# One weight load moved ahead, one chunk's inverse a step later, two periods interleaved, a fourth head product in the last down stage

## The chip, the cores and the metric

The kernel runs on one core of a Trainium2 chip. Its engines work side by side, each through its own queue of instructions in order: TensorE (PE, with PEld for the weight loads), VectorE (DVE), ScalarE (ACT), GpSimd (POOL) and SyncE (SP), which issues the DMA transfers here. The metric is the device time of one execution in microseconds; the time of a kernel is the median of its runs.

## The reference

One layer of a transformer with a spectral mixer, on 8192 tokens of 448 channels. What is computed, cut to its core:

```python
mod = (_silu(c) @ w_mod).reshape(c.shape[0], 6, 1, -1)
sa, ca, ga, sb, cb, gb = (mod[:, n] for n in range(6))
h = _layernorm(x) * (1 + ca) + sa
x = x + ga * spectral(h, w1, b1, w2, b2)   # rfft2 over 1 x 8192, two block-diagonal
                                           # complex layers (4 blocks of 112) with ReLU and
                                           # a soft threshold, irfft2
h = _layernorm(x) * (1 + cb) + sb
x = x + gb * ((_gelu(h @ w_gate) * (h @ w_up)) @ w_down)   # 448 -> 1792 -> 448
```

## The kernel before

**Stages.** The 8192 tokens are 64 rows of 128; the transform is built as 128 x 64 matmuls. The first stage does the modulation, the norm, the forward transform, the two spectral layers and the first half of the inverse transform, whose result goes to memory (`vd<-us`). Everything behind it goes by chunks of two rows (`CB = 2`, 256 tokens), 32 in all. For each chunk there is an `inverse` (second half of the inverse transform; its `v` comes from memory and is split into two parts for the matmul from chunk 3 on, `split_v`), a `residual` with `x`, `stats2`, `rsqrt_part`, `norm2`, `pack` (a cast into two f16 parts) and transposes, and then the feed-forward part.

**Chunks 0 to 7** (`NSTD = 8`) take `NFT = 14` steps of `gate_up` (L1127) each; after every two steps a row of the product gate times up goes through a sum of blocks on POOL (L1176 to L1179) and `quantize` (ACT L1187 for the high f16 part, DVE L1188 for the low). `down(i - 1)` runs inside step 2 of chunk `i`. It is Strassen's seven products of half matrices, each over `NP = 7` tile rows and each with three matmuls per row (high by high, high by low, low by high: L1200 to L1202). While these chunks run, the rows of the down weights are prepared: `load_d8(t)` loads row `t` by three DMAs into a tile `dr`, `down_hi(t)` (ACT, L948) and `down_lo(t)` (DVE, L952) make the two f16 parts `wds[t]`.

**Chunks 8 to 31** use a fast form of the gate and up products too, whose weights `wk` are made on the way and stored to memory. Here the work goes by periods `u`, from `U0 = 56`, seven for a chunk. A period has the matmul stages `stage_a`, `stage_b`, `stage_c` and `stage_d` (all L1362), with `copy_b` (ACT L1390: a result of `stage_a` out of PSUM, on which `stage_b` needs to wait), `seed` (ACT L1394), `gel`, `mult`, `sums` and `quant` steps behind them. `phase` puts a chunk's inverse (`winverse`, L1472 to L1474) and the `down` of the chunk before into one of the seven periods.

**What sets the order.** The kernel is written out by hand: the order of the instructions of each engine is the order of the calls. Tables say which calls stand behind which step: `hooks` (steps 0 to 13 of a chunk, for the chunk one or two later), `second` (chunk 1's own additions), `first` (chunk 0 and, by running step number, what follows), `opening` and `late` (first periods; last `down`). `at(n, "load", ...)` puts a load at step `n` of the first stage. All transfers go through the one SP queue, in order.

**Places that the change touches.** Between the first stage and chunk 0 lies a transition: `inverse(0)`, `residual(0)`, `stats2(0)`, `down_hi(0)`, the Sqrt of `rsqrt0` (L1055) with five small DVE operations (L1057 to L1061), `norm2` (L1076, L1077), `pack_hi`, `pack_lo`, and eight transposes on PE (L1109), then the first `gate_up`. Ahead of it `drain()` ends the first stage, some pools are closed and the pool `cp` is opened in their space: in it lie `n2` (the target of `norm2`), `pk` and the tiles `wds[1]` to `wds[6]`. After `down_lo(0)` the pool `fp` is closed, in whose space `cq` and `cp2` (the homes of `dr`) are opened. At the other end, the last `down` has nothing behind it that PE could do: it works off three head products in cuts of tile rows 0 to 3, 4 and 5, with `late` calls (the last period's `stage_d`, `gel1`, `sums`, `quant`) after each cut, and then the rest.

Of the kernel before, what the change touches and what calls it, by code (L numbers as in the profile page):

```python
# [19 lines left out]
D = 448  # L20
# [4 lines left out]
CB = 2  # L25
# [24 lines left out]
def spectral_geglu(ctx, tc, x, w1, b1, w2, b2, wg, wu, wd, cvec, wmod, cf1, cs2, cmi, cgm, out):  # L50
# [277 lines left out]
    with ExitStack() as bctx:  # L328
# [225 lines left out]
        def at(i, hook, fn, *args):  # L554
            side.setdefault((i, hook), []).append((fn, args))
# [346 lines left out]
        def load_d(t, a, b):  # L902
            dma(a[:, 0:2], wdp[t][:, :, 0:HC])
            dma(a[:, 2], wdp[t][:, 1, HC:])
            dma(b, sd[t])
            draws[t] = a, b
# [66 lines left out]
        at(31, "load", load_v1)  # L973
        for i in range(17, nu - 1):
            step(i)
# [5 lines left out]
    with ExitStack() as cctx:  # L981
        cp = cctx.enter_context(tc.tile_pool(name="cp", bufs=1, side="right"))
        H = 128 * CB
        nxt[0]["n"] = cp.tile([128, CB, D], F32, tag="n2", name="n2")
        pkt = cp.tile([128, NXT * 128], F16, name="pk")
# [10 lines left out]

        def load_d8(t):
            load_d(t, *(cp2.tile([128, n, HC], F32, tag=f"dr{n}", name="dr", bufs=2) for n in (3, 4)))
# [377 lines left out]
        def stage_b(u):  # L1376
            mm(u, RY, S2, T2)
# [69 lines left out]
        def period(u):  # L1447
            on(u, stage_a)
            on(u - 1, seed)
            for fn, *args in held:  # L1450
                fn(*args)
            held.clear()
            on(u - 2, joins)
            on(u - 2, gel3)
            on(u - 4, quant_lo)
            on(u - 2, mult3)
            on(u, copy_b)
# [7 lines left out]
            on(u, stage_b)  # L1465
            on(u, lambda v: after(v, 0))
# [172 lines left out]
        for n, k in enumerate((4, 7, 11, 13)):  # L1639
# [15 lines left out]

        second = {
# [32 lines left out]
            5: [(down_hi, 3)],  # L1689
            6: [(down_lo, 3), (load_d8, 5)],  # L1690
            7: [(down_hi, 4)],
            8: [(down_lo, 4), (load_d8, 6)],
            9: [(down_hi, 5)],
            10: [(down_lo, 5)],
            12: [(down_hi, 6)],
            13: [(down_lo, 6)],
# [8 lines left out]
        S.copy(ga_r[:, HC:], ga[:, HC:D])  # L1705
        down_lo(0, range(1))
# [12 lines left out]
        cq = cctx.enter_context(tc.tile_pool(name="cq", bufs=1))  # L1719
        cctx2 = ExitStack()  # L1720
# [8 lines left out]
        V.tensor_scalar(gb_r, gb_r, ds_d, None, op0=ALU.mult)  # L1729

# [12 lines left out]
        for i in range(NSTD):  # L1743
# [4 lines left out]
            for k in range(NFT):  # L1748
# [3 lines left out]
                if k % 2 == 1 and i + k > 1:  # L1752
                    quantize(*((i, k // 2 - 1) if k > 1 else (i - 1, NP - 1)))
# [25 lines left out]
        quantize(NSTD - 1, NP - 1)  # L1779
# [27 lines left out]
        for u in range(U0, NT_ + 1):  # L1807
# [17 lines left out]
            0: lambda: [on(NT_ - 1, joins), on(NT_ - 1, gel3), on(NT_ - 3, quant_lo), on(NT_ - 1, mult3), on(NT_ - 1, stage_d), on(NT_ - 1, gel1), on(NT_ - 1, mult1), on(NT_ - 2, quant_hi), sums(xs[NT_ - 1], V)],  # L1825
# [79 lines left out]
```

## Time and profile before

| | |
|---|---|
| median of 3 runs | 1902.98 us (1902.56 to 1904.65) |
| profiled execution | 1900.89 us, of it the span 1899.1 us |
| mean granted clock of TensorE | 0.994 |
| first stage | 0 to about 367 us |
| transition | about 367 to 382 us (first `gate_up` at 382.35) |
| chunks 0 to 7 | to about 766 us |
| periods | about 766 to 1877 us |
| last `down` | about 1877 us to the end |

The stage bounds are read from the timeline by the first instruction of `gate_up`, of `stage_a` and of the last `down`. The time of the profiled execution lies 1.79 us above its span, for what the span does not hold. Times in rows are microseconds from the start of the span. A row of a timeline has the start, the duration, the engine, the line, the operation, output and inputs with their shapes, and in brackets the idle time of the engine just before with what ended it.

### The profile page before, as it was taken

The page shows a single profiled execution, that of the slowest core. Times are in us where ns is not written, and L with a number is a line of the kernel's source. Part 1 is how long each engine was busy: PE and PEld are TensorE (multiplying, and loading weights), DVE is VectorE, ACT ScalarE, POOL GpSimd, SP SyncE. Part 2 cuts the span into 40 slices and gives each one's busy share as a digit, 9 for nine tenths or more (in the row PEclk, how much of TensorE's full clock was granted, in tenths as well). Part 3 has the DMA queues.
Part 4 walks back from the last instruction along what each step waited for, and adds up shares of the span by engine and source line. Part 5 has one row for each costly group of instructions (what it writes and reads, how often), then busy time and mean ns, then how long its engine had stood idle before and what let it go on. Part 6 is the DMA issues. An engine that isn't in the chain of part 4 may idle for free.

```text
span 1899.1 us, 56360 instructions
## 1 busy us (share of the span) xinstructions
PE 1853.8 (98%) x23332; PEld 1754.4 (92%) x23332; DVE 1429.7 (75%) x2888; ACT 994.8 (52%) x1844; POOL 1265.3 (67%) x1616
## 2 busy tenths in 40 slices
PE   7899999899999999999999999999999999999998
PEld 3599999878989889899999999999999999999998
DVE  8677788777666667777777777777777777777645
ACT  5687888653444444345554545555454454444443
POOL 3157654256777778677777777777777777777533
PEclk9999999999999999999999999999999999999999
DMA  9999777644543445966666666556666666666651
GB/s 356 316 293 262 204 177 196 183 136 108 127 109 89 104 95 128 270 178 175 176 176 168 167 167 167 167 167 168 172 177 174 169 175 179 173 176 175 155 151 55
DMA packets 380602, 330.49 MB, mean 174 GB/s; under 512 B 110772, under 2 KB 358712, under 8 KB 380344
## 3 DMA queue, kind: packets, MB, share of 16 engines
q1 hardware_dynamic: 380344, 326.87, 62.6%
q8 instruction: 183, 3.00, 0.6%
q14 instruction: 75, 0.61, 0.1%
HBM read 243.32 MB, written 60.10 MB: 160 GB/s over the span
## 4 chain that ended last, share of the span: by engine, by line
PE 80%; DVE 8%; DMA 4%; ACT 3%; SPq 2%; issue 2%; POOL 1%; ACTq 0%; DVEq 0%; POOLq 0%
PE set L1362 37%; PE pgu L1127 11%; PE pdn L1202 6%; PE pdn L1200 6%; PE pdn L1201 6%; PE ps L211 2%; DVE y L472 2%; PE set L1201 2%; PE set L1202 2%; PE set L1200 2%; DVE wk L827 1%; PE set L1472 1%; ACT th L114 1%; DVE st L172 1%; DMA tr<-td 0%
## 5 line engine op out<-in xcount | busy, mean ns | idle before, releaser
L1362 PE MATMUL set<-nt,wk 128*128 128x128 f16 x13104 | 743.9, 220 | 5.6 <-ACT sb L1390 4.2
L1362 PEld LDWEIGHTS <-wk 128*128 128x128 f16 x13104 | 736.9, 98 | 10.5 <-issue 8.2
L1202 PE MATMUL pdn<-wd,ac 128*128 128x224 f16 x1218 | 316.1, 260 | 1.2 <-DVE ac L1437 1.2
L1200 PE MATMUL pdn<-wd,ac 128*128 128x224 f16 x1218 | 316.3, 260 | 0.6 <-ACT ac L1427 0.6
L1201 PE MATMUL pdn<-wd,ac 128*128 128x224 f16 x1218 | 316.1, 260 | 0.0
L1127 PE MATMUL pgu<-nt,wk 128*128 128x256 f16 (+1 forms) x2464 | 270.1, 275 | 4.9 <-DVE x L1168 4.8
L1127 PEld LDWEIGHTS <-wk 128*128 128x128 f16 (+1 forms) x2464 | 226.5, 98 | 47.2 <-issue 20.3
L1411 ACT ACTIVATE gl<-c,dg 128x384 f32<-128x384 f32 x168 | 103.4, 616 | 254.4 <-DVE c L1405 253.4
L1437 DVE SCALAR_TENSOR_TENSOR ac<-x,sa_act,ac 128x896 f16<-128x896 f32 x168 | 211.7, 1260 | 14.4 <-ACT ac L1427 14.3
L1176 POOL TENSOR_TENSOR x<-x 128x128 f32<-128x128 f32 x223 | 131.4, 589 | 124.1 <-DVE x L1168 85.4
L1243 POOL TENSOR_TENSOR o<-u,p 128x224 f32<-128x224 f32 x32 | 21.0, 657 | 263.2 <-DVE u L1242 263.2
L1415 DVE TENSOR_TENSOR x<-c,gl 128x384 f32<-128x384 f32 x168 | 176.7, 1052 | 17.2 <-ACT gl L1411 17.2
L1427 ACT ACTIVATE ac<-x,sa_act 128x896 f16<-128x896 f32 x168 | 173.6, 1033 | 3.4 <-DVE x L1179 0.4
L1179 POOL TENSOR_TENSOR x<-x 128x128 f32<-128x128 f32 x223 | 169.3, 759 | 0.0
L1200 PEld LDWEIGHTS <-ac 128*128 128x128 f16 x1568 | 153.2, 98 | 5.7 <-issue 4.8
L1202 PEld LDWEIGHTS <-ac 128*128 128x128 f16 x1568 | 153.2, 98 | 1.7 <-DVE ac L1437 1.7
L1201 PEld LDWEIGHTS <-ac 128*128 128x128 f16 x1568 | 153.3, 98 | 0.1
L1178 POOL TENSOR_TENSOR x<-x 128x128 f32<-128x128 f32 x223 | 148.4, 665 | 0.0
L1399 DVE TENSOR_TENSOR c<-set,sb 128x512 f32<-128x512 f32 x168 | 115.0, 684 | 36.8 <-PE set L1362 36.8
L1163 ACT ACTIVATE gel<-pgu,dg 128x256 f32<-128x256 f32 x112 | 49.4, 469 | 167.6 <-PE pgu L1127 159.8
L1177 POOL TENSOR_TENSOR x<-x 128x128 f32<-128x128 f32 x223 | 118.7, 532 | 17.5
L472 DVE SCALAR_TENSOR_TENSOR y<-pm,t 64x224 f32<-64x224 f32 x256 | 99.4, 388 | 39.0 <-ACT t L464 35.1
(332 smaller groups left out, 3988.7 us busy)
## 6 DMA issues: line engine op xcount, KB each, us to landing
wk<-wk SPq DMA_DIRECT2D x76, 1024.0 KB, 5.6
wk<-wk SPq DMA_DIRECT2D x76, 768.0 KB
tr<-td SPq DMA_DIRECT2D x64, 224.0 KB, 4.2
vd<-us SPq DMA_DIRECT2D x64, 224.0 KB, 3.0
xx<-in_A_x SPq DMA_DIRECT2D x32, 448.0 KB, 6.3
v<-vd SPq DMA_DIRECT2D x63, 224.0 KB, 6.3
out<-x SPq DMA_DIRECT2D x31, 448.0 KB, 2.6
xt<-in_A_x SPq DMA_DIRECT2D x15, 896.0 KB, 18.0
```

The costliest lines, as they stand in the source:

```text
L472: V.scalar_tensor_tensor(y[ri * 64 : ri * 64 + 64, gi], pv[si, ri], LAM, tv[si, ri], op0=ALU.add, op1=ALU.min)
L1127: T.matmul(pgu[i, t, q][:, pr * H : (pr + 1) * H], ws[rows, n, w, tw], nts[i][rows, tn, :], start=start, stop=stop, skip_group_check=True,)
L1176: e.tensor_tensor(s1, a21, a22, ALU.add)
L1178: e.tensor_tensor(s3, a11, a21, ALU.subtract)
L1179: e.tensor_tensor(s4, a12, s2, ALU.subtract)
L1200: T.matmul(ps, ac[:, 0, ka], w[:, 0, kb], start=n == 0, stop=False)
L1201: T.matmul(ps, ac[:, 0, ka], w[:, 1, kb], start=False, stop=False)
L1202: T.matmul(ps, ac[:, 1, ka], w[:, 0, kb], start=False, stop=n == NP - 1)
L1362: T.matmul(ps2[:, pr, reg * 128 : reg * 128 + 128], slot[:, pr, hl, wt, :], nt[:, xt, :], start=start and j == 0, stop=j == len(terms) - 1 ...
L1415: V.tensor_tensor(xs[u][:, 1::3, :], cts.pop(u)[:, 1], gls.pop(u), ALU.mult)
L1427: S.activation(ac[:, 0], xs[u][:, 0:7], AF.Copy, scale=sa_act[:, t : t + 1])
L1437: V.scalar_tensor_tensor(ac[:, 1], xs.pop(u)[:, 0:7], sa_act[:, t : t + 1], ac[:, 0], op0=ALU.mult, op1=ALU.subtract)
```

## The change

- The two tiles that `down` uses for its intermediate results and the two tiles `gbw` of the first stage now share two tiles in one pool `cq` that is open all the time.
- `load_d8` uses one pool for odd and another for even rows; row 1 is loaded in step 31 of the first stage into the odd one, `drp`. `down_hi(1)` stands just after the copy of `ga_r`; `load_d8(2)` ahead of `load_g(1)` and `load_v(1)`; `down_hi(2)`, `down_lo(1)`, `load_d8(3)`, `down_lo(2)` and `load_d8(4)` just after the transposes. The table `first` has one row less and is a tile ahead.
- POOL fills `n2` with zeros when `cp` is opened.
- In chunk 1 the calls of `hooks` from step 6 on come one step later (`later_by_one`).
- The last two `quantize` calls of chunk 7 move into the second period, behind its `seed`; the first period has only `stage_a` and `copy_b`, and `stage_b` of it stands after `stage_a` of the second.
- In the last `down` a fourth product is among the heads (each head in a bank of its own), the `late` calls stand ahead of a cut's third head in cut 0 and ahead of all heads in cuts 1 and 2, the quantize of the last but one period stands ahead of `gel1`, and the last result block is computed with a POOL multiplication and addition ahead of the last product.

```diff
+        def load_d8(t):
+            load_d(t, *((drp if t % 2 else cp2).tile([128, n, HC], F32, tag=f"dr{n}", name="dr") for n in (3, 4)))
...
-        fctx = ExitStack()
+        cq = ctx.enter_context(tc.tile_pool(name="cq", bufs=1))
+        cctx2, fctx = ExitStack(), ExitStack()
+        drp = cctx2.enter_context(tc.tile_pool(name="drp", bufs=1))
         fp = fctx.enter_context(tc.tile_pool(name="fp", bufs=1))
-        gbw = [fp.tile([112, 4, HC], F32, name=f"gbw{h}") for h in range(2)]
+        shared = [cq.tile([128, 4 * HC], F32, name=f"cq{h}") for h in range(2)]
+        gbw = [t[:112].rearrange("p (k c) -> p k c", k=4) for t in shared]
...
+        at(31, "load", load_d8, 1)
...
         nxt[0]["n"] = cp.tile([128, CB, D], F32, tag="n2", name="n2")
+        G.memset(nxt[0]["n"], 0.0)
...
-            p1, p4, u2, u4 = (cq.tile([128, HC], F32, tag=n, name=n) for n in ("p1", "p4", "u2", "u4"))
-            o = cq.tile([128, CB, D], F32, tag="o", name="o")
+            p1, p4, u2, u4 = (shared[0][:, n * HC : (n + 1) * HC] for n in range(4))
+            o = shared[1].rearrange("p (b c) -> p b c", b=CB)
...
-            heads = [(q, banks(q)) for q in range(3 if last else 2)]
+            heads = [(q, banks(n)) for n, q in ((0, 0), (1, 1), (2, 2), (4, 3))[: 4 if last else 2]]
             cuts = [range(0, 4), range(4, 5), range(5, 6)] if last else [range(0, NP - 1)]
             for n, cut in enumerate(cuts):
-                for q, ps in heads:
+                for m, (q, ps) in enumerate(heads):
+                    if last and m == (0 if n else 2):
+                        mid(n)
                     product(i, ps, q, cut)
-                if last:
-                    mid(n)
...
-            V.tensor_tensor(u4, product(i, banks(4), 3), u2, ALU.add)
+            V.tensor_tensor(u4, product(i, heads[3][1] if last else banks(4), 3, rest if last else range(NP)), u2, ALU.add)
             if not last:
                 mid(2)
+            else:
+                G.tensor_tensor(o12, u4, gb_r[:, HC:], ALU.mult)
+                G.tensor_tensor(o12, o12, x1[:, 0, HC:], ALU.add)
...
             for b, h in ((1, 0), (1, 1), (0, 1)) if last else ((1, None), (0, None)):
+                if last and b == 0:
+                    V.tensor_tensor(p1, p3, gb_r[:, HC:], ALU.mult)
+                    V.tensor_tensor(x1[:, 0, HC:], p1, o12, ALU.add)
+                    dma(ov[:, i * CB, HC:], x1[:, 0, HC:])
+                    continue
...
         def period(u):
             on(u, stage_a)
+            if u == U0:
+                copy_b(u)
+                return
+            if u == U0 + 1:
+                stage_b(U0)
+                copy_b(u)
             on(u - 1, seed)
             for fn, *args in held:
                 fn(*args)
...
+            if u == U0 + 1:
+                stage_b(u)
+                after(U0, 0)
             on(u - 1, stage_c)
...
+        def later_by_one(k):
+            if k < 6:
+                return hooks.get(k, [])
+            return (hooks[k - 1] if k > 6 else []) + (hooks[k] if k == NFT - 1 else [])
...
         first = {
-            1: [(down_hi, 1), (down_lo, 1), (load_d8, 3)],
             2: [(inverse, 1), (residual, 1), (stats2, 1), (rsqrt_part, 1, 9)],
-            3: [(down_hi, 2)],
-            4: [(pack_hi, 1), (pack_lo, 1), (down_lo, 2), (load_d8, 4)],
...
+            3: [(down_hi, 3)],
+            4: [(pack_hi, 1), (pack_lo, 1), (down_lo, 3), (load_d8, 5)],
...
         S.copy(ga_r[:, HC:], ga[:, HC:D])
+        down_hi(1)
         down_lo(0, range(1))
...
+        load_d8(2)
         load_g(1)
         load_v(1)
-        for t in (1, 2):
-            load_d8(t)
...
         V.tensor_scalar(gb_r, gb_r, ds_d, None, op0=ALU.mult)
+        down_hi(2)
+        for t in (1, 2):
+            down_lo(t)
+            load_d8(t + 2)
...
+                if (i, k) == (NSTD - 1, NFT - 1):
+                    held += [(quantize, i, t) for t in range(NP - 2, NP)]
+                elif k % 2 == 1 and i + k > 1:
...
-                for d, fn, *args in (hooks if i < NSTD - 2 else soon).get(k, []):
+                for d, fn, *args in later_by_one(k) if i == 1 else (hooks if i < NSTD - 2 else soon).get(k, []):
```

How the change moves instructions is shown at three places. The first is ACT in the transition, from the last copies of the first stage to the casts of `pack_hi`; `wd` is a row of the down weights, `r` the reciprocal root, `pk` the packed norm. Before:

```order
L506 COPY us<-pi_5731 128x448
L948 ACTIVATE wd_3371<-raw,dsc 128x672
L948 ACTIVATE wd_3371<-raw,dsc 128x896
L1705 COPY ga_r<-psm 128x224
L1055 ACTIVATE r_3375<-mv_3374,eps 128x2
L1056 ACT_TABLE_LOAD
L1056 ACTIVATE g_3377<-mv_3374 128x2
L1082 CAST pk<-n_5748 128x448 x2
```

And now:

```order
L506 COPY us<-pi_5742 128x448
L951 ACTIVATE wd_3371<-raw,dsc 128x672
L951 ACTIVATE wd_3371<-raw,dsc 128x896
L1731 COPY ga_r<-psm 128x224
L951 ACTIVATE wd_5762<-dr,dsc 128x672
L951 ACTIVATE wd_5762<-dr,dsc 128x896
L1060 ACTIVATE r_3375<-mv_3374,eps 128x2
L1061 ACT_TABLE_LOAD
L1061 ACTIVATE g_3377<-mv_3374 128x2
L1087 CAST pk<-n_5759 128x448 x2
```

Two activations on row 1 of the down weights (`wd_5762`, a tile of `cp`) have come in between the copy of `ga_r` and the Sqrt.

The second place is DVE in the second half of chunk 1, where `x` is the product of gate and up, `ac` its low part, `x_3372` the residual of chunk 3 and `cst` its statistics. Before:

```order
L1577 SCALAR_TENSOR_TENSOR ws<-wr,sww,ws 128x3x128
L1037 TENSOR_TENSOR x_3372<-pi_6854,ga_r 128x448
L1037 TENSOR_TENSOR x_3372<-pi_6858,ga_r 128x448
L1168 TENSOR_TENSOR x_6932<-pgu,gel 128x2x128
L1577 SCALAR_TENSOR_TENSOR ws<-wf,sww,ws 128x3x128
L1046 BN_STATS cst_6940<-x_3372 128x6 x2
L1049 BN_AGGR cmv<-cst_6940 128x2 x2
L1168 TENSOR_TENSOR x_6932<-pgu,gel 128x2x128
L1188 SCALAR_TENSOR_TENSOR ac<-x_6892,sa_act,ac 128x896
```

And now:

```order
L1601 SCALAR_TENSOR_TENSOR ws<-wr,sww,ws 128x3x128
L1173 TENSOR_TENSOR x_6928<-pgu,gel 128x2x128
L1601 SCALAR_TENSOR_TENSOR ws<-wf,sww,ws 128x3x128
L1042 TENSOR_TENSOR x_3372<-pi_6898,ga_r 128x448
L1042 TENSOR_TENSOR x_3372<-pi_6902,ga_r 128x448
L1173 TENSOR_TENSOR x_6928<-pgu,gel 128x2x128
L1193 SCALAR_TENSOR_TENSOR ac<-x_6884,sa_act,ac 128x896
L1051 BN_STATS cst_6981<-x_3372 128x6 x2
L1054 BN_AGGR cmv<-cst_6981 128x2 x2
```

The residual has moved behind a multiplication, and the statistics behind the next multiplication and quantize.

The third place is ACT in the first two periods. `ac` are the quantizes of chunk 7's last two rows, `sb` the target of `copy_b`, `vh` a split of the next chunk's `v`, and the copies within `set` are `seed`. Before:

```order
L1163 ACTIVATE gel<-pgu,dg 128x256 x2
L1187 ACTIVATE ac<-x_11248,sa_act 128x896
L1187 ACTIVATE ac<-x_11287,sa_act 128x896
L1390 COPY sb<-set_11336 128x512
L114 CAST vh<-v 128x896
L1394 COPY set_11336<-set_11336 128x2x128
L1333 CAST pk_11341<-n_11262 128x192
L1333 CAST pk_11341<-n_11262 128x256 x2
L1390 COPY sb<-set_11337 128x512
```

And now:

```order
L1168 ACTIVATE gel<-pgu,dg 128x256 x2
L1403 COPY sb<-set_11300 128x512
L114 CAST vh<-v 128x896
L1403 COPY sb<-set_11301 128x512
L1407 COPY set_11300<-set_11300 128x2x128
L1192 ACTIVATE ac<-x_11218,sa_act 128x896
L1192 ACTIVATE ac<-x_11257,sa_act 128x896
L1346 CAST pk_11305<-n_11232 128x192
L1346 CAST pk_11305<-n_11232 128x256 x2
```

Both copies of `copy_b` and the first `seed` now stand ahead of the two quantizes. On PE, in step with that, `stage_a` of the second period (32 matmuls) stands between `stage_a` and `stage_b` of the first.

More of the change, by code (lines that the diff above doesn't have):

```diff
@@ L995, in x8 @@
             return cp.tile([128, 8, 128], F32, tag="x8", name="x8", bufs=3)
-        def load_d8(t):
-            load_d(t, *(cp2.tile([128, n, HC], F32, tag=f"dr{n}", name="dr", bufs=2) for n in (3, 4)))
         def each(i):
@@ L1456, in period @@
             on(u - 2, mult3)
-            on(u, copy_b)
+            if u != U0 + 1:
+                on(u, copy_b)
             on(u - 2, stage_d)
@@ L1463, in period @@
             on(u - 3, quant_hi)
+            if u == U0 + 1:
+                stage_b(u)
+                after(U0, 0)
             on(u - 1, stage_c)
-            on(u, stage_b)
+            if u != U0 + 1:
+                on(u, stage_b)
             on(u, lambda v: after(v, 0))
@@ L1684, in spectral_geglu @@
         first = {
-            1: [(down_hi, 1), (down_lo, 1), (load_d8, 3)],
             2: [(inverse, 1), (residual, 1), (stats2, 1), (rsqrt_part, 1, 9)],
-            3: [(down_hi, 2)],
-            4: [(pack_hi, 1), (pack_lo, 1), (down_lo, 2), (load_d8, 4)],
[L1689 to L1696, printed above, removed]
+            3: [(down_hi, 3)],
+            4: [(pack_hi, 1), (pack_lo, 1), (down_lo, 3), (load_d8, 5)],
+            5: [(down_hi, 4)],
+            6: [(down_lo, 4), (load_d8, 6)],
+            7: [(down_hi, 5)],
+            8: [(down_lo, 5)],
+            9: [(down_hi, 6)],
+            10: [(down_lo, 6)],
         }
@@ L1718, in spectral_geglu @@
         fctx.close()
-        cq = cctx.enter_context(tc.tile_pool(name="cq", bufs=1))
-        cctx2 = ExitStack()
         cp2 = cctx2.enter_context(tc.tile_pool(name="cp2", bufs=1))
+        load_d8(2)
         load_g(1)
         load_v(1)
-        for t in (1, 2):
-            load_d8(t)
         S.copy(gb_r, gb[:, :D])
@@ L1778, in spectral_geglu @@
                         fn(i + d, *args)
-        quantize(NSTD - 1, NP - 1)
         assert not prep and not first and not ahead
@@ L1824, in spectral_geglu @@
         late = {
-            0: lambda: [on(NT_ - 1, joins), on(NT_ - 1, gel3), on(NT_ - 3, quant_lo), on(NT_ - 1, mult3), on(NT_ - 1, stage_d), on(NT_ - 1, gel1), on(NT_ - 1, mult1), on(NT_ - 2, quant_hi), sums(xs[NT_ - 1], V)],
+            0: lambda: [on(NT_ - 1, joins), on(NT_ - 1, gel3), on(NT_ - 3, quant_lo), on(NT_ - 1, mult3), on(NT_ - 1, stage_d), on(NT_ - 2, quant_hi), on(NT_ - 1, gel1), on(NT_ - 1, mult1), sums(xs[NT_ - 1], V)],
             1: lambda: [on(NT_ - 2, quant_lo), on(NT_ - 1, quant_hi)],
```

1 line of the change is left out of this document (removed).

## The prediction

> **What bounds the kernel now.** I read the page's busy shares first (busy us, share, instructions), then the list of waits on TensorE (line waiting, engine and line waited for, total us, times, longest), then for each place the timelines of the engines and the windows around it.
>
> ```profile
> PE 1853.8 (98%) x23332; PEld 1754.4 (92%) x23332; DVE 1429.7 (75%) x2888; ACT 994.8 (52%) x1844; POOL 1265.3 (67%) x1616
> PE pgu L1127 <- DVE x L1168: 4.8, 4, 2.4
> PE ptr L1109 <- ACT pk L1082: 4.4, 2, 3.5
> PE set L1362 <- ACT sb L1390: 4.2, 1, 4.2
> PE pdn L1202 <- DVE ac L1437: 1.2, 2, 1.0
> ```
>
> TensorE is busy for 98% of the span, so this change, which adds and removes no matmul, can win only PE's idle time and half-clock time. The rows show the idle time that it could reach: waits of single places, 14.6 us in all, not a loop's. I therefore go place by place, in the order of the program, and ask when PE's next matmul can start.
>
> **The transition (ACT and DVE timelines, then PE, before chunk 0).** Columns: start, duration, then in brackets the idle time ahead and what ended it.
>
> ```profile
> 368.86 1.79 ACT L948 ACTIVATE wd<-raw,dsc 128x672 f16<-128x672 f32 x2
> 374.19 0.29 ACT L1055 ACTIVATE r<-mv,eps 128x2 f32<-128x2 f32 x1 [3.14 <-DVE mv L1049]
> 375.31 0.16 DVE L1061 TENSOR_TENSOR r<-r,t 128x2 f32<-128x2 f32 x1
> 376.16 0.68 DVE L1076 SCALAR_TENSOR_TENSOR n<-x,mv,cb_r 128x448 f32<-128x448 f32 x1 [0.69 <-DMA g<-cgm]
> 378.34 0.23 PE L1109 MATMUL ptr<-ident,pk 128*128 128x128 f16 x1 [3.48 <-ACT pk L1082]
> 382.35 1.06 PE L1127 MATMUL pgu<-nt,wk 128*128 128x256 f16 x4
> L315 POOL MEMSET ones<- 128x258 f32 x1 | 0.3, 313 | 0.0
> ```
>
> Before, the reciprocal root was ready at 375.31+0.16 = 375.47 (1.28 after the Sqrt started) and the norm waited 0.69 more, to 376.16, for the transfers that the new pool's space had to be free of. Now ACT has the two `down_hi(1)` activations ahead of the Sqrt. They write a tile of that same new pool, so they are subject to that same release; ACT runs in order, so the Sqrt is queued behind them, and behind it the DVE chain, the norm, the casts, the transposes and `gate_up`. With the release at 376.16 and the durations of `down_hi(0)`: 376.16 + 1.79 = 377.95, Sqrt, + 1.28 = 379.23 for the norm: 3.1 later. The memset (128x896) is bounded by 313 ns below and 313·896/258 = 1.09 us above, on POOL from the release on; it ends by 377.25 and is hidden behind the ACT chain. If ACT's wait were already over when it came to it, only the memset would remain: +0.3 to +1.1, I take +0.85. If the memset came ahead of ACT's work as well, +4.0. I take **+3.1**, since the order puts the write ahead of the Sqrt and a release can't be passed. PE's transposes run at half clock before; 3.1 is nearly the length of a clock window (3.41 below), so I take the half-clock part as shifted, not longer.
>
> The other side of it: `down_lo(1)` and `down_lo(2)` move from the first steps to just after the transposes, and `load_d8(2)` goes ahead of `load_g(1)` and `load_v(1)` on SP.
>
> ```profile
> 380.20 1.15 DVE L952 SCALAR_TENSOR_TENSOR wd<-raw,dsc,wd 128x896 f16<-128x896 f32 x1
> 373.93 2.27 SPq L921 DMA_DIRECT2D v<-vd  x2
> 381.44 0.37 SPq L903 DMA_DIRECT2D dr<-in_B_w_down  x1
> 382.84 0.43 SPq L903 DMA_DIRECT2D dr<-in_B_w_down  x1
> v<-vd SPq DMA_DIRECT2D x4, 224.0 KB, 5.7
> 391.31 1.67 PE L1021 MATMUL pi<-v,g 128*128 128x448 f32 x4
> ```
>
> `dr` of row 2 lies on space that `down_lo(0)` frees: 380.20 + 1.15 + 3.1 = 384.45. Three issues take 1.40 (381.44 to 382.84), g and xx between 0.43 and 1.13 each (the issues of dr and of v), I take 1.3 for both, the two v 2.27: the second v is issued near 388.3 and lands 5.7 later, 394.0 (5.7 is the median in the DMA view of 372 to 395). `inverse(1)` wants it 391.31 − 382.35 = 8.96 after the first `gate_up`, now 394.4. So it is just hidden: **0**, and up to the whole lateness if it isn't (a rival below). The early `load_d8(1)`, three issues before the last stores, falls where PE still works on the inverse (to 374.9): 0, and if the stores were pushed, its 784 KB (448, 224 and 112) at the 205 GB/s of the row for 471.38 below are 3.8 us.
>
> **Chunk 0.** The second product waits here; DVE has the residual chain, then a quantize and `down_lo(2)`.
>
> ```profile
> 406.49 1.69 PE L1127 MATMUL pgu<-nt,wk 128*128 128x256 f16 x14 [1.94 <-DVE x L1168]
> ```
>
> `down_lo` here now belongs to row 3, one tile ahead, in the same step, so the wait stays except for a little DVE time freed earlier: **−0.3**, between 0 and −1.9.
>
> **Chunk 1.** Everything that the hooks do for chunk 3 comes one step later from step 6 on.
>
> ```profile
> 452.73 2.40 POOL L116 TENSOR_TENSOR v<-v,vh 128x896 fp32r<-128x896 f32 x1
> 455.19 0.47 PE L1028 MATMUL pi<-v,gh 128*128 128x448 f32 x1 [0.96 <-POOL v L116]
> 469.38 0.63 DVE L1046 BATCH_NORM_STATS2 cst<-x 128x6 f32<-128x448 f32 x1 [0.48 <-POOL x L1038]
> 470.14 0.39 DVE L1168 TENSOR_TENSOR x<-pgu,gel 128x256 f32<-128x256 f32 x1
> 470.58 2.72 PE L1127 MATMUL pgu<-nt,wk 64*128 64x256 f16 x16 [2.41 <-DVE x L1168]
> 464.55:467.96 3.41, 3.41 (x34) 2.83 (x32) 3.41 (x6) 1.04 (x1) 3.33 (x6) 1.00 0.40 86
> 467.96:471.38 3.42, 1.01 (x11) 0.51 (x8) 2.94 (x7) 0.47 (x2) 2.16 (x2) 0.99 0.62 144
> 471.38:474.79 3.41, 3.41 (x19) 2.47 (x17) 3.06 (x15) 1.41 (x3) 1.81 (x4) 0.51 1.21 205
> ```
>
> Two waits stand here. PE's 0.96 is for the POOL split (2.40) of the next chunk's inverse; with the inverse a step later it goes. The 2.41 is `x` at 470.14 queued behind the BN_STATS, which wait for POOL's adds; with the stats a step later the multiplication is ahead of them. The windows (busy us of PE, PEld, DVE, ACT, POOL, then granted clock, DMA share, GB/s) add a second cost: after a window with PE busy 1.01 of 3.42 the next one ran at 0.51, about 3.41·0.5 = 1.7 us of work lost. DVE, however, is full: 3.41 of 3.41 in 464.55, and 2.94 in the next with its own wait of 0.48, so the work that steps back collides with what stands a step later. Bounds: −1.0 (only the split's) and −0.96−2.41−1.7 = −5.1. In the new order the stats come after one more quantize, and a step later a pair of multiplications stands behind the residual; I leave 2.1 of waits there, without a half-clock window, **−3.0**.
>
> The Trainium skill, "TensorE: Matmul & The Clock Gate", section "🔬 Part 1: The HAM clock gate (the "warmup" mystery)", says that the clock halves after at least one idle window of about 3.4 us. The trace agrees on the window's length, but the half clock came after 2.41 us of idling with 1.01 busy; by the rule 1.7 would not belong to this term, the sum would be −3.6 and the time 1899.4.
>
> **The first two periods.**
>
> ```profile
> 766.08 1.95 PE L1362 MATMUL set<-nt,wk 128*128 128x128 f16 x32
> 770.66 1.04 ACT L1187 ACTIVATE ac<-x,sa_act 128x896 f16<-128x896 f32 x1 [1.63 <-POOL x L1179]
> 771.61 0.56 ACT L1390 COPY sb<-set 128x512 f32<-128x512 f32 x1
> 772.23 10.10 PE L1362 MATMUL set<-nt,wk 128*128 128x128 f16 x154 [4.20 <-ACT sb L1390]
> 771.75:775.17 3.42, 2.94 (x29) 2.94 (x29) 3.38 (x3) 2.19 (x5) 2.08 (x1) 0.51 1.10 336
> 782.13 0.45 PE L1472 MATMUL set<-vh,gh 128*128 128x448 f32 x1
> 764.50 20.70 SPq L1278 DMA_DIRECT2D wk<-wk  x8
> wk<-wk SPq DMA_DIRECT2D x6, 1024.0 KB, 10.9
> ```
>
> PE waits 4.20 for `copy_b`, which stands on ACT behind two such quantizes that wait for POOL; then 2.94 busy at half clock, 1.47 lost. The quantizes now come after the seed and PE has `stage_a` of the next period to do. The 154 matmuls take 9.90 − 1.47 = 8.43, 0.055 each. So `stage_a(U0+1)` runs 768.0 to 769.9 over `copy_b`; then two `stage_b` (10 each) around the second copy (769.9 + 0.56) to 771.1, `stage_c(U0)` (24) to 772.5. What is late next is the weight of `stage_a(U0+2)`, the first of the eight issues at 764.50, with transfers at 336 GB/s: at the median 10.9 it lands at 775.4; shorter if the queue ahead is. I take 10.0: 774.5. The 78 matmuls left take 4.3, `winverse` starts at 778.8 instead of 782.13: **−3.3**. Ends: −2.4 (10.9) and −5.2 (no wait). A wait of 2.0 in a window that has 1.4 busy may still halve the clock; 1.94 before 406.49 did not (14 matmuls in 1.69), so I leave that out of the sum.
>
> **The last down.**
>
> ```profile
> 1882.93 0.27 PE L1200 MATMUL pdn<-wd,ac 128*128 128x224 f16 x1 [0.59 <-ACT ac L1427]
> 1884.32 0.27 PE L1202 MATMUL pdn<-wd,ac 128*128 128x224 f16 x1 [1.02 <-DVE ac L1437]
> 1885.52 0.27 PE L1202 MATMUL pdn<-wd,ac 128*128 128x224 f16 x1 [0.16 <-DVE ac L1437]
> 1894.80 0.65 POOL L1215 TENSOR_TENSOR x<-o,x 128x224 f32<-128x224 f32 x1
> 1895.74 0.39 DVE L1215 TENSOR_TENSOR x<-o,x 128x224 f32<-128x224 f32 x1
> ```
>
> A fourth head product brings 12 matmuls (0.096 each) forward, 1.2 us of cover, and `stage_d` with all behind it goes 12 earlier: 0.59 + 1.02 + 0.16 = **−1.8** (bounds −0.6, the ACT wait alone, and −1.8). One DVE operation (0.39) leaves the very end, but the SP queue still passes the store behind POOL's add (1895.45) first: 0. The shared tiles only give slices other names: 0.
>
> **Sum.** 3.1 − 0.3 − 3.0 − 3.3 − 1.8 = −5.3. The profiled run took 1900.89 (span 1899.1, 1.79 around it), 2.09 under the median of 1902.98; −5.3 gives 1895.6 for it and **1897.7** for the median.
>
> **Rivals.**
> 1. The transition costs no more than the memset (+0.85): −7.5, 1895.4. For it: ACT was idle for 3.14 ahead of the Sqrt. Against: the release comes after that idle time.
> 2. Every wait goes: +0.85 − 1.9 − 5.1 − 5.2 − 1.8 = −13.2, 1889.8. Against: DVE at 3.41 of 3.41, the 336 GB/s.
> 3. Chunk 1's wait moves and only the split's 1.0 is won: −3.3, 1899.7. For: the full DVE.
> 4. Slower than before: v of chunk 1 lands late. At the 10.9 of the first periods it lands at 388.3 + 10.9 = 399.2, 4.8 after 394.4, and a half-clock window adds 1.7: −5.3 + 6.5 = +1.2, 1904.2. It decides from a landing at 398.0 on (3.6 late and 1.7). For: three transfers of `dr` go ahead in the queue. Against: 5.7 in this window.
>
> **How the numbers follow.** Forecast 0.42, rivals 0.14, 0.10, 0.16, 0.12, and 0.06 for others, half of them slower. 0.2% (3.8 us) is what a measurement can tell from no change: faster is under 1899.2, slower over 1906.8. Forecast's own range 1895 to 1900, two thirds of it faster (0.28); rivals 1 and 2 faster (0.24); rival 3 nearly all within; rival 4 from 1902 to 1909, half of it slower. Faster 0.53, same 0.36, slower 0.11. The range runs from 1892, most of rival 2's left out, to 1904.5.
>
> **What would show it.** After: Sqrt near 378 behind `down_hi(1)`, first `gate_up` near 385.5; no wait of L1028's kind on POOL in chunk 1, a smaller one on `x`, clock 1.0 there; no 4.2 wait on `copy_b`, but some 2 us on a weight transfer at 772; `winverse` 3 us earlier against the chunks; none of the three waits in the last down. Wrong if the norm starts within 1 us of its old place, if `inverse(1)` waits, or if a half-clock window stands at 775.

## The result, and the profile after

The changed kernel takes 1897.15 us (median of 9 runs, 1895.44 to 1899.12), the kernel before 1902.98 (9 runs, 1901.44 to 1904.65): a ratio of 0.997, 95% interval 0.996 to 0.998. The profiled execution of the changed kernel took 1896.69 us with a span of 1894.9, 4.2 less than the span before.

The page's busy shares after, the same row as the prediction's first:

```profile
PE 1853.1 (98%) x23332; PEld 1755.2 (93%) x23332; DVE 1428.9 (75%) x2887; ACT 995.1 (53%) x1844; POOL 1266.2 (67%) x1619
```

Every engine has as good as the same work; only waits have moved. The list of PE's waits after (line waiting, engine and line waited for, total us, times, longest):

```profile
PE ptr L1114 <- ACT pk L1087: 6.5, 2, 5.5
PE pgu L1132 <- DVE x L1173: 3.7, 5, 1.9
PE set L1375 <- DMA wk<-wk: 1.6, 1, 1.6
PE set L1375 <- ACT sb L1403: 0.7, 1, 0.7
```

Against the rows before: the wait in the transition grew (4.4 to 6.5), that on `copy_b` fell from 4.2 to 0.7, a new one of 1.6 is for weights, and those on the POOL split (`pi L1028`) and on `ac` (`pdn L1202`) are gone.

To see where the 4.2 us came from, I follow PE from landmark to landmark, since each instruction of PE comes in the same order in nearly all of these kernels. The rows of the PE timeline that serve as landmarks (start, duration, operation), before as far as the prediction doesn't show them:

```profile
371.66 3.19 PE L686 MATMUL psm<-gbw,cs 112*128 112x224 f32 x16
424.32 0.92 PE L1021 MATMUL pi<-v,g 128*128 128x448 f32 x2
507.63 0.45 PE L1026 MATMUL pi<-vh,gh 128*128 128x448 f32 x1
1875.19 2.17 PE L1362 MATMUL set<-nt,wk 128*128 128x128 f16 x36 [0.56 <-DVE c L1405]
1894.17 0.26 PE L1202 MATMUL pdn<-wd,ac 128*128 128x224 f16 x1
```

And after:

```profile
372.61 3.19 PE L686 MATMUL psm<-cq,cs 112*128 112x224 f32 x16
385.38 9.58 PE L1132 MATMUL pgu<-nt,wk 128*128 128x256 f16 x68
394.79 1.67 PE L1026 MATMUL pi<-v,g 128*128 128x448 f32 x4
427.14 1.29 PE L1026 MATMUL pi<-v,g 128*128 128x448 f32 x3
508.73 0.45 PE L1031 MATMUL pi<-vh,gh 128*128 128x448 f32 x1
767.18 0.89 PE L1375 MATMUL set<-nt,wk 128*128 128x128 f16 x13
780.25 0.45 PE L1496 MATMUL set<-vh,gh 128*128 128x448 f32 x1
1873.29 0.89 PE L1375 MATMUL set<-nt,wk 128*128 128x128 f16 x13 [0.56 <-DVE c L1418]
1889.97 0.26 PE L1207 MATMUL pdn<-wd,ac 128*128 128x224 f16 x1
```

| stretch, from start to start | before | after | difference |
|---|---|---|---|
| first stage, to its last block of 16 matmuls | 371.66 | 372.61 | +0.95 |
| transition, to the first `gate_up` | 10.68 | 12.76 | +2.08 |
| to `inverse(1)` | 8.96 | 9.42 | +0.46 |
| to `inverse(2)` | 33.01 | 32.34 | −0.67 |
| chunk 1 and what follows, to `inverse(4)` | 83.31 | 81.59 | −1.72 |
| to the first `stage_a` | 258.45 | 258.45 | 0 |
| first periods, to `winverse` | 16.05 | 13.06 | −2.99 |
| to the last 195 matmuls | 1093.06 | 1093.04 | −0.02 |
| last `down`, to the last matmul | 18.98 | 16.69 | −2.29 |
| last matmul to the end of the span | 4.93 | 4.94 | +0.01 |

A half-clock window is a stretch of some 3.4 us in which the granted clock of TensorE reads about 0.5 and matmuls start at double spacing. The difference in the first row of the table can't be told from what such windows do: with the same work on PE there, it lies between 371.30 and 374.02 in all the runs below. The spread arises in the first 107 us (the granted clock from 60 to 90 us is anything from 0.83 to 1.00); from there on all traces take 266.4 to 266.6 us. Without that row the change brings −5.1 us in this trace. Where no clock and no transfer enters, the landmarks repeat to a tenth of a microsecond or better (258.45 in all fourteen traces, 16.69 in all eleven with the whole new last `down`), so they tell effects of tenths of a microsecond apart, which one time of a run cannot.

### The profile page after: what moved, and what is told of

Same layout as the page of the kernel before. It is cut to its first block, busy times and chain, and to the rows that moved or that the text cites. A ratio compares the mean times of both kernels' runs of the same rounds, so it can differ in the third digit from the quotient of the medians.

```text
span 1894.9 us, 56358 instructions
## 1 busy us (share of the span) xinstructions
PE 1853.1 (98%) x23332; PEld 1755.2 (93%) x23332; DVE 1428.9 (75%) x2887; ACT 995.1 (53%) x1844; POOL 1266.2 (67%) x1619
## 4 chain that ended last, share of the span: by engine, by line
PE 81%; DVE 9%; DMA 4%; ACT 2%; SPq 1%; issue 1%; POOL 1%; ACTq 0%; DVEq 0%; POOLq 0%
PE set L1375 34%; PE pgu L1132 11%; PE pdn L1207 6%; PE pdn L1205 6%; PE pdn L1206 6%; PE ps L211 2%; PE set L1207 2%; PE set L1206 2%; PE set L1205 2%; DVE y L472 1%; DVE x L1428 1%; DVE c L1412 1%; DVE wk L827 1%; DMA raw<-in_B_w_gate 1%; DVE tf L1316 1%
## 5 line engine op out<-in xcount | busy, mean ns | idle before, releaser
L1251 POOL TENSOR_TENSOR cq<-cq 128x224 f32<-128x224 f32 x32 | 21.0, 657 | 262.8 <-DVE cq L1250 262.8
```

## The experiments

All are edits of the changed kernel. The stretches named in the expectations are those of the table.

**`down_hi(1)` out of the Sqrt's way, with and without the memset.**

```diff
         S.copy(ga_r[:, HC:], ga[:, HC:D])
-        down_hi(1)
...
-        down_hi(2)
         for t in (1, 2):
+            down_hi(t)
+        for t in (1, 2):
             down_lo(t)
```

and, in the second kernel, also `-        G.memset(nxt[0]["n"], 0.0)`.

> The changed kernel with one part undone: down_hi(1) stands behind the transposes, ahead of down_hi(2), the memset stays. Measured as the transition, from the start of the last block of 16 matmuls of L686 to the first gate_up: 10.69 us before the change (371.66 to 382.35), 12.77 with it (372.61 to 385.38). Theory: the two activations that waited for the release hold up the Sqrt, so without them the norm starts right after the memset, 376.02 + 0.84 plus some 0.1 against 379.19: 10.5. Rival: the release of the space sets everything that comes after it, wherever the activations stand: 12.8.

> As hi1_late, and without the memset of n2. Theory: with ACT out of the way the memset is what the norm waits for, so that its 0.84 us go as well: transition 9.7 us. Rival: the memset lies beside the release and is hidden anyway: 10.5, the same as hi1_late.

Measured: 10.93 and 10.04 us (one run each, 1893.24 and 1894.71; before on the same chip 1901.0). Both theories hold in direction; each gave a transition 0.3 to 0.4 too short. The ACT timeline of the changed kernel shows the mechanism:

```profile
375.99 1.79 ACT L951 ACTIVATE wd<-dr,dsc 128x672 f16<-128x672 f32 x2 [4.03 <-DMA vd<-us]
377.68 0.28 ACT L1060 ACTIVATE r<-mv,eps 128x2 f32<-128x2 f32 x1
```

ACT stands idle for 4.03 us at the first activation of `down_hi(1)`, until the last store lands, and the Sqrt comes out behind both. With them moved, the Sqrt ran at 374.29 in that run, 2.48 after the start of the last PE block against 5.07 with the change. The memset, however, costs in another way than I expected. From the first kernel, the DVE chain behind the Sqrt, and POOL; the last row is the same `TENSOR_SCALAR` in the kernel without the memset, whose lines count one lower:

```profile
375.01 0.16 DVE L1064 SCALAR_TENSOR_TENSOR t<-mv,t 128x2 f32<-128x2 f32 x1
375.21 0.91 DVE L1065 TENSOR_SCALAR t<-t 128x2 f32<-128x2 f32 x1
376.15 0.16 DVE L1066 TENSOR_TENSOR r<-r,t 128x2 f32<-128x2 f32 x1
376.56 0.69 DVE L1081 SCALAR_TENSOR_TENSOR n<-x,mv,cb_r 128x448 f32<-128x448 f32 x1 [0.24 <-issue]
375.25 0.84 POOL L992 MEMSET n<- 128x896 f32 x1 [8.55 <-DVE t L1064]
375.59 0.17 DVE L1064 TENSOR_SCALAR t<-t 128x2 f32<-128x2 f32 x1
```

The norm did not wait for the memset (its idle time of 0.24 is there without the memset too): beside the memset a DVE operation on two elements per partition took 0.91 instead of 0.17. That is 0.74 of the 0.89 between the two kernels.

**The loads of chunk 1 ahead of row 2 again.**

```diff
-        load_d8(2)
         load_g(1)
         load_v(1)
+        load_d8(2)
```

> The changed kernel with load_g(1) and load_v(1) ahead of load_d8(2) on SP again, all else as changed. Theory: the last store landed 3.1 us after its issue with the change and 3.9 before it because those four loads no longer follow it into the DMA queue; with them back the release comes some 0.8 later and the transition takes 13.6 us; inverse(1) comes 9.4 after the first gate_up as now, since its v was in time both ways. Rival: the store's landing has nothing to do with the loads: transition 12.8; or v(1) was late with the change, and inverse(1) now comes earlier than 9.4 after gate_up.

Measured: transition 13.45. The release of ACT, from the ACT timeline of this kernel:

```profile
376.97 1.79 ACT L951 ACTIVATE wd<-dr,dsc 128x672 f16<-128x672 f32 x2 [4.71 <-DMA vd<-us]
```

That is 4.06 after the start of the last PE block (372.91) against 375.99 − 372.61 = 3.38 with the change. So with the four loads behind the stores the release comes 0.68 later. It is no scatter: in the eight kernels with the transition of the change it comes 3.38 to 3.43 after that block. `inverse(1)` came 8.23 after `gate_up`, earlier than the 9.4 that I gave; not for its data, though, since PE waits for no transfer at `inverse(1)` in any of these kernels. In the eight kernels with the transition of the change the same stretch is 8.24 to 9.67 long, and PE waits for nothing in it; the difference is how many matmuls fall into the half-clock stretch that starts it (10 to 23 at double spacing).

**The inverse alone in its old step.**

```diff
             if k < 6:
                 return hooks.get(k, [])
-            return (hooks[k - 1] if k > 6 else []) + (hooks[k] if k == NFT - 1 else [])
+            if k == 6:
+                return hooks[6]
+            return (hooks[k - 1] if k > 7 else []) + (hooks[k] if k == NFT - 1 else [])
```

> The changed kernel with the inverse of chunk 3 back in step 6 of chunk 1, its residual and all behind it still a step later. Measured from inverse(2) to inverse(4): 83.31 us before (424.32 to 507.63), 81.59 with the change (427.14 to 508.73). Theory: the 1.90 us wait at 461.05, with the half-clock window behind it, stands where the six matmuls of the inverse used to cover DVE's norm; with them back there that wait goes, the 0.96 for the POOL split returns, and the multiplication stays ahead of the statistics: 79.0, between 78.6 and 79.6. Rival: DVE is full in this chunk, so a wait as long comes up a few steps later: 81.6 or more.

Measured: 81.29. The theory fell and the rival's cause held: a wait as long came up later. Its 81.6 includes the half-clock window; the other runs without one there have 81.30 and 81.29. PE's waits from 425 to 490 in this kernel:

```profile
PE pi L1033 <- POOL v L116: 0.9, 1, 0.9
PE pgu L1132 <- DVE x L1173: 0.9, 1, 0.9
PE pdn L1207 <- DVE ac L1193: 0.6, 1, 0.6
```

One wait of 1.9 with a half-clock window has become three of 2.4 together without one, and the stretch is as long as in the kernels that keep the one wait without the window. Where PE waits is a matter of order; that DVE's work sets the length is what the next runs test.

**The hooks of chunk 1 in their old steps.**

```diff
-                for d, fn, *args in later_by_one(k) if i == 1 else (hooks if i < NSTD - 2 else soon).get(k, []):
+                for d, fn, *args in (hooks if i < NSTD - 2 else soon).get(k, []):
```

> The changed kernel with later_by_one undone, the hooks of chunk 1 in their old steps. Measured from inverse(2) to inverse(4): 83.31 us before; 81.59 with the change and 81.3 in the runs without a half-clock window there. Theory: the step's shift alone made this gain, so 83.3 returns, with the 0.96 on the POOL split and a wait of 2.4 on the multiplication behind the statistics. Rival: DVE is full in this stretch whatever its order, and the gain came from the down weights being ready a tile ahead: 81.3 stays.

Measured: 83.30, with waits of 0.94 and 2.41 in the old places. The step's shift alone is worth the 1.7 (with a half-clock window) to 2.0 (without) of this stretch.

**Two weight forms out of the full stretch.**

```diff
             ("m2", forms_hi, 1, 3),
-            (3, forms_lo, 1, 3),
+            ("m2", forms_lo, 1, 3),
```

> The changed kernel with two DVE operations (the low parts of two weight forms, 1.54 us together at 454.45 with the change) called at the end of down in step 2 of chunk 1 instead of in step 3, where DVE waits for pdn between its operations. Theory: from 449 to 482 DVE has no idle time but what it waits for the high parts, so that stretch sets the time of chunk 1 and any work taken out of it shortens it: from inverse(2) to inverse(4) 81.3 - 1.5 = 79.8, and the 1.9 wait at 461 falls to 0.4. Rival: PE waits there for the place in the order and not for DVE's sum of work, or the later waits (0.9 and 0.6 with the inverse in its old step) come back: 81.0 or more.

Measured: 80.62, and the wait at 461 fell from 1.90 to 1.27 only. Taking out 1.54 us of DVE work brought 0.7. Neither case as written: the operations behind the moved ones stayed long or became longer, the norm's second one 2.39 where the transition has it at 0.69. They still lay beside POOL's work, which named the next theory:

```profile
455.33 2.39 DVE L1082 SCALAR_TENSOR_TENSOR n<-n,rcy,sb_r 128x448 f32<-128x448 f32 x1
454.77 2.46 POOL L116 TENSOR_TENSOR v<-v,vh 128x896 fp32r<-128x896 f32 x1
```

**The POOL splits of chunk 3 out of it.**

```diff
-                if i == 1 and k == 3:
-                    split_g(3)
-                    split_v(3)
...
+                if (i, k) == (1, 2):
+                    split_g(3)
+                    split_v(3)
                 if k == 2 and i > 0:
                     down(i - 1, two_banks, lambda n: steps_std(i, n))
```

> The changed kernel with the splits of chunk 3's g and v (POOL 0.77 and 2.39 at 454.80, and their ACT casts) called ahead of down in step 2 of chunk 1, where POOL is idle from 437 to 446, instead of in step 3. Theory: DVE's norm is slow at 456.24 (2.16 and 1.30 against 0.68 and 0.69 in the transition) because POOL works beside it, so POOL's sum of work counts in this stretch like DVE's own; with the splits gone from there the norm takes some 1.8 less and the 1.9 wait at 461 all but goes: from inverse(2) to inverse(4) 79.5, between 79.2 and 80.0. Rival: the norm's length has nothing to do with POOL and the DVE operations keep their durations: 81.3. A third case, in which the later waits at 481 and 487 come back as with the inverse in its old step: 80.3 to 81.0.

Measured: 79.43; the wait before the inverse is gone, 0.24 at 479 and 0.57 at 486 are left. Rows of DVE and POOL of the changed kernel beside each other:

```profile
456.24 2.16 DVE L1081 SCALAR_TENSOR_TENSOR n<-x,cmv,cb_r 128x448 f32<-128x448 f32 x1
458.44 1.30 DVE L1082 SCALAR_TENSOR_TENSOR n<-n,rcy,sb_r 128x448 f32<-128x448 f32 x1
460.58 0.42 DVE L1173 TENSOR_TENSOR x<-pgu,gel 128x256 f32<-128x256 f32 x1
455.53 2.39 POOL L116 TENSOR_TENSOR v<-v,vh 128x896 fp32r<-128x896 f32 x1
457.88 1.38 POOL L1565 TENSOR_TENSOR wr<-wr,wf 128x384 f32<-128x384 f32 x1
```

and the same DVE operations with the split moved:

```profile
455.82 0.67 DVE L1081 SCALAR_TENSOR_TENSOR n<-x,cmv,cb_r 128x448 f32<-128x448 f32 x1
456.52 0.69 DVE L1082 SCALAR_TENSOR_TENSOR n<-n,rcy,sb_r 128x448 f32<-128x448 f32 x1
458.05 0.41 DVE L1173 TENSOR_TENSOR x<-pgu,gel 128x256 f32<-128x256 f32 x1
```

The norm's two operations take 1.36 instead of 3.46, and the multiplication that PE waits for comes 1.8 earlier against `inverse(2)`. In the changed kernel the first of the norm's operations ended at 458.40 and the second at 459.74, each 0.48 after the POOL instruction beside it: they were held until POOL was done. In its new place the split holds DVE as well, an operation of 0.17 for 2.01, but there PE waits for none of it:

```profile
435.34 2.01 DVE L127 TENSOR_SCALAR rcy<-rcy 128x2 int32<-128x2 int32 x1
435.25 2.08 POOL L116 TENSOR_TENSOR v<-v,vh 128x896 fp32r<-128x896 f32 x1
```

**g and xx behind the weights in the last standard chunk.**

```diff
                 if k == 9 and i > 0:
                     load_v(i + 3)
+                if k == (11 if i == NSTD - 1 else 9) and i > 0:
                     load_g(i + 3)
```

> The changed kernel with g and xx of chunk 10 (576 KB) loaded behind the weights of the third period on SP instead of ahead of them, in the last standard chunk. Measured from the first stage_a matmul to winverse: 16.05 us before, 13.06 with the change. Theory: the 1.63 wait before the third stage_a is that for its weights, in a full queue (about 340 GB/s), so with 576 KB less ahead of them they land 1.7 us earlier: 11.5, between 11.2 and 12.0. Rival: that stage is held by the DMA's mean rate, the next weights are then as late, or the half-clock returns: 13.0 or more.

Measured: 14.08, in the rival's range, but that can't be told from kernels without this edit, which take 12.82 to 14.32. The waits of PE from 766 to 783 say more:

```profile
PE set L1375 <- ACT sb L1403: 2.2, 1, 2.2
PE set L1375 <- DVE c L1418: 0.8, 1, 0.8
```

The wait for the weights is gone, as the theory has it; but PE waits 2.2 for the second `copy_b`, which stands on ACT behind the split of v (`vh`). In the changed kernel this already showed:

```profile
770.74 0.94 ACT L114 CAST vh<-v 128x896 fp32r<-128x896 f32 x1 [0.99 <-DMA v<-vd]
771.59 0.58 ACT L1403 COPY sb<-set 128x512 f32<-128x512 f32 x1
```

So two transfers, v and the weights, are awaited by two engines, while the DMA moves 339 to 353 GB/s (765 to 780 us of the changed kernel). ACT's wait for v is 2.52 here and 0.16 to 2.19 in the kernels with the same loads in the old order, so the late v need not be the edit's doing; what sets it stays open.

**The first periods and the last down as before.** The edit takes back the diff's pieces in `period`, in the quantize of chunk 7, in `down` and in `late`.

> The changed kernel with the first periods and the last down as before. Two places far apart are read in one run. Theory: from the first stage_a matmul to winverse 16.05 again (13.06 with the change), and from the last winverse-free point, the 195th matmul from the end, to the last matmul 18.98 (16.69 with the change), with waits of some 0.6, 1.0 and 0.2 in the last down. Rival: part of either gain came from earlier work that the change moved away from these places: 13 to 15 and 17 to 18.5.

Measured: last `down` 18.98, the theory's number. The first periods took 17.51, more than theory and rival gave and more than before the change: the wait of 4.18 is there, and PE ran at half clock longer behind it. The windows of this kernel (busy us of PE, PEld, DVE, ACT, POOL, granted clock, DMA share, GB/s):

```profile
771.50:775.00 3.50, 0.00 (x0) 0.00 (x0) 1.68 (x2) 1.87 (x4) 1.96 (x3) 0.88 1.07 355
775.00:778.40 3.40, 3.34 (x32) 3.34 (x32) 3.37 (x3) 1.77 (x5) 2.34 (x1) 0.50 1.10 335
778.40:781.80 3.40, 3.40 (x42) 3.40 (x40) 2.47 (x6) 1.29 (x3) 2.99 (x6) 0.62 1.10 339
```

The same wait cost 1.5 us more than in the trace before. Against the 12.82 to 14.32 of the twelve kernels that have the interleaving, it is worth 1.7 to 4.7 us. The whole run took 1905.23 us, more than the kernel before on the same chip (1902.41, one run each): this trace also has the longest first stage of all, 374.02.

**The fourth head without the earlier calls.**

```diff
-                for m, (q, ps) in enumerate(heads):
-                    if last and m == (0 if n else 2):
-                        mid(n)
+                for q, ps in heads:
                     product(i, ps, q, cut)
+                if last:
+                    mid(n)
```

with the old order in `late`.

> The changed kernel with the fourth head product of the last down, but with the late calls in their old places and order. Measured from the 195th matmul from the end to the last: 18.98 us before, 16.69 with the change. Theory: the head adds only 3 matmuls (0.29 us) of cover per tile row behind stage_d, 0.86 over three rows, and the rest of the gain is that stage_d and what hangs on it start earlier: 18.1. Rival: the fourth head is the cover that was missing and the order of the calls adds nothing: 16.7.

Measured: 18.40, nearer the theory's 18.1. Of the 2.29 gained, 0.58 are the head's, and 1.71 come from `stage_d` and what hangs on it being called earlier, with the new order in `late`.

**What worked, together.** `down_hi(1)` behind the transposes and the early splits, without and with the memset:

> The changed kernel with three edits from the runs above together: down_hi(1) behind the transposes, no memset, the splits of chunk 3 ahead of down in step 2 of chunk 1. Theory: the gains lie at different places and add up: transition 10.0 instead of 12.8, inverse(2) to inverse(4) 79.4 instead of 81.5; 1897.15 - 2.7 - 2.0 = 1892.4 us median, between 1891.4 and 1893.6. Rival: what the transition gains is given back by a longer half-clock stretch behind it, as in the single run without the memset (first gate_up to inverse(1) 9.7 against 8.7): 1894 or more.

> As best, but with the memset. Theory: the memset costs what it took from DVE's chain in the transition, 0.9: 1893.3 us median and 10.9 for the transition. Rival: it is given back by the clock: the same as best within 0.4.

Measured: 1891.64 us (5 runs, 1890.56 to 1895.55) and 1891.85 (1891.50 to 1893.17), against 1903.5 before on the same chip (9 runs, 1901.41 to 1906.59): ratios 0.9938 (0.9923 to 0.9953) and 0.9938 (0.9926 to 0.9951). Both are faster than the kernel before, and more so than the changed kernel, whose ratio on its own chip is 0.997 (0.996 to 0.998); the three were not run side by side. The transitions are 10.03 and 10.95, chunk 1 79.44 in both: the gains add up. The memset's 0.9, plain at the landmark, is not seen in the medians (0.2 apart, ranges overlapping), as the rival of the second run has it. From `gate_up` to `inverse(1)`, the half-clock stretch behind it, the two profiled runs take 9.48 without and 8.94 with the memset; whether the clock gives the 0.9 back on average stays open.

## Why the prediction was right

The forecast was 1897.7 us for the median, and 1897.15 came. On the profiled run it was −5.3 against −4.2, of which +0.95 lies in the first stage. The places and most of the causes were right, but that −5.3 and the −5.1 behind the first stage agree so closely is luck: the terms were off by −1.0, +0.5, −0.4, +1.3, +0.3 and −0.5, and these cancelled.

- **Transition, +3.1: mechanism right, size off; +2.08.** The Sqrt stood behind the two activations and they behind the release, as the two ACT rows show, and taking them out gave back 1.83. The step that failed is "With the release at 376.16": I took the old time of the norm's start for that of the release, and as fixed. The loads that the change puts behind `down_lo(0)` had been running against the very stores that were awaited; without them the release came earlier, by 0.68 as the run with the loads back shows. The old 376.16 is 4.50 after the last PE block, 0.44 more than the 4.06 of that run; 0.24 of it is the idle time that DVE shows ahead of this operation even where it waits for nothing, the rest stays open. The memset was indeed hidden in the change itself (376.02 to 376.86, beside the activations).
- **`inverse(1)` and its v, 0: right.** The two v were issued from 386.81 on, a microsecond before what I had worked out, and PE did not wait.
- **Half clock there, "shifted, not longer":** 0.46 longer in this trace, and anything from 0.7 shorter to 0.7 longer in the runs with the same instructions. It could not be told from the order.
- **Chunk 0, −0.3: −0.67.** The wait fell from 1.94 to 1.07, and one of 0.32 is new a little later.
- **Chunk 1, −3.0: −1.72.** Both waits went, as predicted, and DVE kept one, as predicted (1.9, where I left 2.1). What failed is "without a half-clock window", with the 1.7 that it put into the sum, and the place. PE stopped ahead of the inverse, not at the statistics, for a multiplication behind the norm that POOL had stretched; and the clock halved for a window in five of the seven kernels that have this wait. That window itself cost only 0.3 (81.6 against 81.3): the two kernels without it wait 0.27 and 0.57 later on, the five with it don't. The bound of −5.1, everything gone, was too far: with no wait left but 0.24 and 0.57, the stretch took 79.43, 3.9 less than before. In a stretch that another engine sets, as here, a half-clock window was not worth its own 1.7.
- **First periods, −3.3: −2.99 here.** The next thing late was the weights of the third `stage_a`, as predicted: 1.63 instead of 2.0. Not foreseen was 0.67 on the second `copy_b`, behind a cast that waits for v. No half-clock window stood at 775 (1.00 from 775 to 780). Over the twelve kernels with the new periods the stretch is 12.8 to 14.3, so against the one trace before the gain is anything from 1.7 to 3.2.
- **Last down, −1.8: −2.29.** The mechanism held (none of the three waits is left), the size was too small by a misreading of the column: the idle time before a matmul counts from the modelled end of the one ahead (0.26 long), but the next one normally starts 0.096 after its start. From start to start the three waits are 0.85, 1.28 and 0.42 in place of 0.096 each, 2.26 together, not 1.77.
- **The tail, 0: right.** 4.93 us from the last matmul to the end before, 4.94 after.

PE's waits after in chunk 0, in chunk 1 and in the first periods:

```profile
409.10 3.11 PE L1132 MATMUL pgu<-nt,wk 128*128 128x256 f16 x27 [1.07 <-DVE x L1173]
461.05 0.48 PE L1132 MATMUL pgu<-nt,wk 64*128 64x256 f16 x5 [1.90 <-DVE x L1173]
772.22 2.06 PE L1375 MATMUL set<-nt,wk 128*128 128x128 f16 x34 [0.67 <-ACT sb L1403]
775.91 4.53 PE L1375 MATMUL set<-nt,wk 128*128 128x128 f16 x78 [1.63 <-DMA wk<-wk]
```

The rule of the Trainium skill that was weighed ("TensorE: Matmul & The Clock Gate", section "🔬 Part 1: The HAM clock gate (the "warmup" mystery)") would not have the clock halved by 2.41 us of idling. The runs differ from it and go with the row: the window from 461.0 ran at 0.58 after a wait of 1.90,

```profile
457.60:461.00 3.40, 1.55 (x15) 0.97 (x13) 3.33 (x6) 1.22 (x3) 2.25 (x3) 1.00 0.00 0
461.00:464.50 3.50, 3.45 (x15) 2.46 (x15) 3.50 (x5) 1.64 (x5) 3.42 (x5) 0.58 0.77 156
```

and in two runs (`down_hi(1)` moved, and the loads ahead again) the same wait of 1.9 did not do it: the granted clock behind it reads 1.00. So with waits near 2 us it went either way here. Of the rivals, the third, that the wait of chunk 1 moves, holds half of the truth: 1.9 of 3.4 moved.

## What to carry to other kernels

In this kernel an instruction that writes into a freshly opened space inherits the wait for the transfers that still use the space (4.03 us of ACT); such an instruction belongs behind the short chain that everyone waits for, not ahead of it, and it pays to see which transfers compete with the ones that free the space. When a wait goes and another of nearly the same length appears, add up the work of the engine waited for over the whole stretch, and look for operations of it that are longer there than elsewhere and for what runs beside them (POOL beside DVE here), before moving anything again. Measure such edits from landmark to landmark of the trace: effects of 0.3 us were plain there, where nine times of one kernel spread over 3.7.

## What the runs showed of the hardware

- Some DVE operations stood still while POOL worked: a norm of 0.68 took 2.16 beside a POOL instruction of 2.39, and an operation on two elements per partition took 0.91 instead of 0.17 beside a memset of 0.84. The Trainium skill, "SBUF — State Buffer", section "🔬 SBUF: two separate sides", says that DVE and GpSimd share a pair of ports that one of them holds for its whole instruction while the other blocks, if the DVE operation runs in a 2-port mode or has two SBUF inputs against a GpSimd operation that reads SBUF. The norm's rows (two inputs, beside a POOL subtraction that reads `v` and `vh`) agree; the memset reads nothing, so its row would need the 2-port mode, which no run here shows.
- A wait of 1.9 us of PE was followed by a half-clock window in five kernels (the changed one: 0.58) and not in two (1.00). The same code behind the transition took 8.24 to 9.67 us, with no wait of PE in it, by the clock.
- The last store landed sooner when no load followed it into the queue: the release came 3.38 to 3.43 us after the last PE block began in eight kernels, 4.06 in the one with four loads behind the stores.
